# One activation table set for Ln and Exp, a bf16 maximum in the softmax shift, and a new sequence of tasks

## The chip, the cores and the metric

The kernel runs on one core of a Trainium2 chip. The time is that of one execution on the device, in microseconds (us); the profile shows one execution of its own and gives its span, from the first instruction to the last. The engines are PE (matrix products; PEld are its weight loads), DVE (elementwise and reductions), ACT (one function of a table, with scale and bias, per instruction), POOL and SP. SP, POOL and ACT also issue DMAs, each in its own queue. ACT holds one set of function tables at a time; an ACT_TABLE_LOAD instruction changes it, and the program's builder puts one in front of an activation whose function the loaded set lacks.

## The reference

The input x is 2048 rows of 640. Two results are mixed by a gate of each row.

```python
def reference(A_x, A_wqkv, A_wo, ..., B_log_dt, B_Dskip, gate_w):
    # A: attention, 32 heads of 20, each position sees 8 positions at distance 0, 2, ..., 14
    qkv = (x @ wqkv).reshape(B, S, 3, H, Dh)
    logits = einsum("bhsd,bhswd->bhsw", q, kg) * scale
    logits = where(mask, logits, -1e9)
    attn = softmax(logits, axis=-1)
    a = einsum("bhsw,bhswd->bhsd", attn, vg).reshape(B, S, D) @ wo
    # B: a diagonal state space model as a long convolution
    dt = exp(log_dt)[:, None]
    P = exp((dt * A)[:, :, None] * arange(L))       # A complex, 640 x 192
    K = einsum("dn,dnl,dn->dl", Cc, P, dt * Bc).real
    b = irfft(rfft(x padded) * rfft(K padded)) + x * Dskip
    g = sigmoid((x * gate_w).sum(-1))
    return g * a + (1 - g) * b
```

## The kernel before

**Tasks and order.** The work is cut into tasks: 1264 in a plan "main" and 304 in a plan "tail". A task has a name, the engines that can do it, its dependences, and a function that issues its instructions. `ORDER` holds, for each plan, a string of steps from one task's number to the next; a letter after a step (A, D, S, G for ACT, DVE, SP, POOL) chooses the engine where a task may run on two. `Plan.emit` issues the tasks in that sequence, and ties each instruction behind the one before it on its engine. So the string is the program order of every engine and queue, and an engine that waits at a task holds up all that stands behind it. Each task carries a duration for whoever searched the sequence; at run time it has no effect.

**Stages of main.** First (to about 46 us) the parameters. `SSMParams.build` loads C, B, A and log_dt and makes, on [128, 960] tiles, the logarithm of a size and a phase for each of 640 x 192 modes: the products of C and B (`weights`), log and square root by Ln and Exp (`size`, `half`), an arctangent, then a sum (stt_at) and a conversion to integers (fix_t0, L722). Ten results (pieces 0 to 9) are cut to bf16 by tasks mk0 to mk9 and stored to the DRAM tensor Sprm by sp0 to sp9, on SP or POOL. The pieces are tiles pc of a pool of four buffers, taken in turn: the fifth piece made takes the first one's buffer, and so waits until that one's store has landed. When all ten have landed, `KGen.load_L` loads them back as matrices L (queue of SP, the first half also ACT's). In the same stretch SP's queue loads x, wqkv and A; the last two of these loads transpose x (L183) and come, in program order, before any task of SP. PE transposes the other half of x (turn, evicted by tev) and computes q, k and v (late0 to late59, evicted by lev, on ACT or DVE).

Next, the stream (about 46 to 205 us). `KGen.plan` makes K in ten chunks: PE forms angles and exponents (arg, L828), ACT takes the sine (L843) and the exponential (L845), DVE multiplies (pq, L865 and L867), PE sums (kmm, L883). Between them runs attention in eight blocks (`plan_core`): products (prod, L381), logits into PSUM (lg), the maximum over 8 positions (max, L403), its subtraction (neg, L411), the exponential (exp, L415), the sum and division (sum, at), a trip through DRAM to spread the weights (ast, asb on SP), the weighted values (pv, L455), and the output projection (wo, ga). Sine and exponential lie in different table sets, so ACT changes tables between them.

Then K is spread out through DRAM (own, other, then xst and xld on SP and POOL), and the first steps of the Fourier transforms follow: f1 and fk of K, fu of x, each with an eviction of 1024 columns (f1e, fke, fue) from the two PSUM buffers "ar". The tail does the rest of the transforms (fp, sp, products, inv, cp), mixes with the gate and stores.

**The softmax shift.** The logits of a block lie in a PSUM tile lg. DVE takes the maximum mx in f32, and splits -mx into two bf16 tiles, hi (L406) and lo (L407). PE adds both to lg, as two matmuls with the identity (L411). The shift is the same for all 8 positions of a softmax.

Of the kernel before, what the change touches and what calls it, by code (L numbers as in the profile page):

```python
# [11 lines left out]
ALU = mybir.AluOpType  # L12
AX = mybir.AxisListType
F32 = mybir.dt.float32
BF16 = mybir.dt.bfloat16
# [6 lines left out]
D = 640  # L22
# [18 lines left out]
def _attn_consts():  # L41
# [123 lines left out]
class Attn:  # L165
# [86 lines left out]
    def consts(self, cst):  # L252
# [7 lines left out]
        def small():  # L260
            nc.gpsimd.dma_start(self.ind[:], nc.inline_tensor(ind_np, name="c_ind").ap())
            nc.gpsimd.dma_start(self.mask0[:], nc.inline_tensor(mask0_np, name="c_mask0").ap())
# [1171 lines left out]
```

## Time and profile before

| | us |
|---|---|
| three runs | 316.70, 318.62, 317.23 |
| median | 317.23 |
| span of the profiled execution | 315.8 |
| busy PE, DVE, ACT, POOL in it | 288.0, 290.1, 288.5, 55.9 |
| table loads on ACT in it | 18 of 1.283 each |

The profiled execution is not one of the three runs. Its span is 1.4 us below their median; the times of the runs include what lies around the span, and a run differs from the next by up to 1.9 us. Busy means that at least one instruction of the engine was under way; matrix products are pipelined and their ends modelled, so a busy PE isn't PE at its peak. In a timeline row the first two numbers are the start from the span's beginning and the length; a bracket gives the idle time before it and what ended it. SPq and POOLq are the queues in which these engines issue DMAs. In a row of the costliest groups, the numbers behind the bar are busy us, mean ns of one, and idle us before it. In the windows, the columns behind the stretch are its length and the busy us of PE, PEld, DVE, ACT and POOL with the number of instructions, the granted clock of PE, the busy share of the DMA engines and GB/s.

### The profile page before, as it was taken

What the parts mean: (1) busy time and instruction counts of PE and PEld (TensorE: products, weight loads), DVE (VectorE), ACT (ScalarE), POOL (GpSimd) and SP (SyncE); (2) the same over time, 40 slices, a digit from 0 to 9 for tenths busy, and PEclk for the clock granted to TensorE, in tenths of its full rate; (3) what the DMA queues carried; (4) which work ended last, traced back from release to release, by engine and by line L of the source; (5) the groups of instructions that cost most, each with busy time, mean ns of one, the idle gap of its engine ahead of it and who ended that gap; (6) DMA issues with size and microseconds to landing.
All of it is one profiled execution on the core that took longest, in us unless ns stands there. A gap on an engine that the chain in (4) does not pass through costs nothing. (4 is left out here: it accounts for less than half of the span.)

```text
span 315.8 us, 12097 instructions
## 1 busy us (share of the span) xinstructions
PE 288.0 (91%) x5276; PEld 169.2 (54%) x5276; DVE 290.1 (92%) x403; ACT 288.5 (91%) x429; POOL 55.9 (18%) x83
## 2 busy tenths in 40 slices
PE   8899998999999999999998999879989999996840
PEld 3556444445554454546554555446667776656730
DVE  4999999999999999999999999988878799999881
ACT  4999869999999999999999999979987899998890
POOL 8631133200100001111032022040010000000063
PEclk9999999999999999999999999978999999999995
DMA  7995546773412204634698595771192453983066
GB/s 256 366 254 140 153 103 175 167 169 98 91 35 54 69 10 133 130 111 130 187 255 183 110 227 140 139 193 41 66 324 79 153 181 105 196 165 57 4 154 180
DMA packets 47150, 45.67 MB, mean 145 GB/s; under 512 B 27018, under 2 KB 40634, under 8 KB 47098
## 3 DMA queue, kind: packets, MB, share of 16 engines
q1 hardware_dynamic: 40776, 26.68, 33.1%
q0 software_dynamic: 5360, 17.50, 22.1%
q8 instruction: 41, 0.67, 1.0%
q10 hardware_dynamic: 962, 0.73, 0.7%
q14 instruction: 11, 0.09, 0.1%
HBM read 29.57 MB, written 14.01 MB: 138 GB/s over the span
## 5 line engine op out<-in xcount | busy, mean ns | idle before, releaser
L316 PE MATMUL tb<-bufA 128*128 128x512 bf16 x300 | 74.5, 383 | 1.6 <-DMA bufA<-in_A_wqkv_dram 0.8
L843 ACT ACTIVATE big<-ar 128x740 bf16<-128x740 int16 (+1 forms) x72 | 56.9, 858 | 2.4 <-PE ar L828 2.0
L828 PE MATMUL ar<-Rarg,L 64*128 64x212 bf16 (+4 forms) x600 | 48.7, 254 | 4.5 <-ACT big L843 3.0
L845 ACT ACTIVATE big<-ar 128x848 bf16<-128x848 f32 x60 | 50.5, 915 | 0.3 <-PE ar L828 0.2
L455 DVE TENSOR_TENSOR pv<-vc,asb 128x2048 bf16<-128x2048 bf16 x40 | 47.3, 1221 | 1.3 <-DMA asb<-aS 1.3
L316 PEld LDWEIGHTS <-bufA 128*128 128x128 bf16 x300 | 31.7, 120 | 30.0 <-issue 9.1
L828 PEld LDWEIGHTS <-L 64*128 64x128 bf16 x600 | 21.1, 95 | 33.5 <-issue 30.2
L865 DVE TENSOR_TENSOR pt<-big 128x1024 bf16<-128x1024 bf16 x48 | 32.3, 704 | 0.2
L883 PEld LDWEIGHTS <-pt 128*32 128x32 bf16 (+1 forms) x2560 | 23.1, 92 | 11.5 <-issue 8.8
L883 PE MATMUL kps<-qq,pt 128*32 128x21 bf16 (+1 forms) x2560 | 27.8, 175 | 0.8 <-issue 0.8
L486 PE MATMUL tb<-wo_sb,oT 128*128 128x320 bf16 x160 | 27.3, 301 | 0.0
L381 DVE TENSOR_TENSOR prod<-qA,kA 128x2048 bf16<-128x2048 bf16 x20 | 23.6, 1221 | 0.3 <-PE lg L387 0.3
L381 DVE TENSOR_TENSOR prod<-prj 128x2048 bf16<-128x2048 bf16 x20 | 23.8, 1221 | 0.0
L462 PE MATMUL tb<-pv,ind 128*64 128x512 bf16 (+1 forms) x192 | 23.2, 360 | 0.3 <-DVE pv L455 0.3
L513 ACT ACTIVATE sp_k<-fp 128x640 bf16<-128x640 f32 x31 | 22.4, 877 | 0.8 <-PE fp L1096 0.8
L513 ACT ACTIVATE sp_u<-fp 128x640 bf16<-128x640 f32 x29 | 21.6, 894 | 0.2 <-PE fp L1096 0.2
L867 DVE TENSOR_TENSOR qq<-big 128x1344 bf16<-128x1344 bf16 x24 | 21.3, 887 | 0.0
L374 POOL DMA_DIRECT2D vc<-vS x16 | 11.5, 722 | 53.2 <-DVE pv L455 49.0
L1214 POOL DMA_DIRECT2D out_dram<-ot x14 | 7.7, 558 | 69.4 <-ACT tt L1193 68.0
L1096 PEld LDWEIGHTS <-PHI 128*128 128x128 bf16 x160 | 15.5, 97 | 7.8 <-issue 1.3
L486 PEld LDWEIGHTS <-oT 128*128 128x128 bf16 x160 | 13.3, 98 | 8.1 <-issue 3.5
L513 ACT ACTIVATE big<-bp 128x1024 bf16<-128x1024 f32 x14 | 13.9, 1025 | 3.5 <-PE bp L1326 3.3
(177 smaller groups left out, 534.0 us busy)
## 6 DMA issues: line engine op xcount, KB each, us to landing
vc<-vS POOLq DMA_DIRECT2D x16, 327.5 KB, 5.3
gaS<-ga SPq DMA_DIRECT2D x8, 320.0 KB
Usb<-in_A_x_dram POOLq DMA_DIRECT2D x8, 320.0 KB, 4.7
gaF<-gaS SPq DMA_DIRECT2D x8, 320.0 KB
bufA<-in_A_wqkv_dram SPq DMA_DIRECT2D x3, 800.0 KB
L<-Sprm SPq DMA_DIRECT2D x76, 30.0 KB
asb<-aS SPq DMA_DIRECT2D x16, 128.0 KB
psi<-c_psi SPq DMA_DIRECT2D x4, 512.0 KB
```

The lines of the kernel that those rows point to most:

```text
L316: nc.tensor.matmul(ppf, self.wq[:, which, kt, e::5], self.xT[:, c0 // 1024, kt, c0 % 1024:c0 % 1024 + SC], start=(kt == 0), stop=(kt == NK ...
L381: nc.vector.tensor_tensor(b[e][:], q[:, e, o:o + C].unsqueeze(1).to_broadcast([128, W, C]), win(k[:, e, :], o, W, DIL, C), ALU.mult)
L455: nc.vector.tensor_tensor(o, vw, b["asb"][:].unsqueeze(2).to_broadcast(sh), ALU.mult)
L462: nc.tensor.matmul(b["op", e][64 * a:64 * a + 64, 0:n, :], ind[:, 32:96], b["pv", e][:, w, a, 0:n, :], start=(w == 0), stop=(w == 3), skip ...
L486: nc.tensor.matmul(apf[:, :320], b["oT"][:, e, i * 128:(i + 1) * 128], wo_sb[:, e, hf * 320:(hf + 1) * 320], start=(e == 0), stop=(e == 4))
L513: nc.scalar.activation(o, i, ACT.Identity)
L828: nc.tensor.matmul(ar[:, g2, a0:a0 + ncol], L[rows, sb, gv, l0:l0 + 128], R[rows, c0:c0 + ncol], start=True, stop=True, tile_position=(64 ...
L843: nc.scalar.activation(d_[:, :, s0 * QW:s1 * QW], ar[:].bitcast(I16)[:, :, 0:2 * (s1 - s0) * QW:2], ACT.Sin, scale=SCL)
L845: nc.scalar.activation(dst[:, gp::2].rearrange("p g s n -> p g (s n)"), ar[:, :, 0:2 * EW], ACT.Exp)
L865: nc.vector.tensor_tensor(pt[:, :, k, :], gg[:, :, ::-1] if k else gg, e1, ALU.mult)
L867: nc.vector.tensor_tensor(qq[:], trg[:, :, KI:].rearrange("p a (v m) -> p a v m", v=2), exq[:, :, KI:].unsqueeze(2).to_broadcast([128, 32, ...
L883: nc.tensor.matmul(kps[32 * g:32 * g + 32, h, NM * ql:NM * ql + NM], pt[rows, k, v, :], qq[rows, k, v, :], start=(g not in started), stop= ...
```

## The change

Three things are changed.

First, the program loads the set that holds both Ln and Exp before its first activation. The builder keeps a set as long as it serves.

Second, the maximum is written in bf16, and this rounded value is subtracted by one matmul with a negated identity, a constant that is loaded on POOL's queue at the start. A shift that is common to all positions of a softmax cancels, so rounding it does not change the result.

Third, both strings of `ORDER` are new, for the same tasks. The durations that the tasks carry for max and neg are changed with them.

```diff
@@ class Attn: def consts
         self.ident = cst.tile([128, 128], BF16, name="ident")
+        self.minus = cst.tile([128, 128], BF16, name="minus")
...
             nc.gpsimd.dma_start(self.mask0[:], nc.inline_tensor(mask0_np, name="c_mask0").ap())
+            nc.gpsimd.dma_start(self.minus[:], nc.inline_tensor((-ident_np.astype(np.float32)).astype(NPBF), name="c_minus").ap())
@@ class Attn: def plan_core
-                mx = wk.tile([128, 64], F32, name="mx", bufs=1)
-                nc.vector.tensor_reduce(mx[:], lg[:].rearrange("p w t -> p t w"), AX.X, ALU.max)
-                b["hi"] = wk.tile([128, 64], BF16, name="hi", bufs=1)
-                b["lo"] = wk.tile([128, 64], BF16, name="lo", bufs=1)
-                nc.vector.tensor_scalar(b["hi"][:], mx[:], -1.0, None, ALU.mult)
-                nc.vector.scalar_tensor_tensor(b["lo"][:], mx[:], -1.0, b["hi"][:], ALU.mult, ALU.subtract)
+                b["mx"] = wk.tile([128, 64], BF16, name="mx", bufs=1)
+                nc.vector.tensor_reduce(b["mx"][:], lg[:].rearrange("p w t -> p t w"), AX.X, ALU.max)
...
-                for k in ("hi", "lo"):
-                    nc.tensor.matmul(b["lg"][:], ident[:], b[k][:].unsqueeze(1).to_broadcast([128, W, 64]), start=False, stop=(k == "lo"), skip_group_check=True)
+                nc.tensor.matmul(b["lg"][:], self.minus[:], b["mx"][:].unsqueeze(1).to_broadcast([128, W, 64]), start=False, stop=True, skip_group_check=True)
...
-            mx = pl.add(f"max{sc}", "D", 1.09, top, deps=[l])
-            ng = pl.add(f"neg{sc}", "P", 0.435, lower, deps=[mx], eq=1024)
+            mx = pl.add(f"max{sc}", "D", 0.65 if sc else 0.9, top, deps=[l])
+            ng = pl.add(f"neg{sc}", "P", 0.216, lower, deps=[mx], eq=512)
@@ class SSMParams: def build
         lnd = pin.tile([128, 5], F32, name="lnd")
+        nc.scalar.preload_act_table_set("natural_log_exp_and_others")
         nc.scalar.activation(dtb[:], ldt[:], ACT.Exp)
```

The strings are long and can't be read as they stand. Decoded with the tasks' numbers, the sequence of the parameter stage is, on ACT and DVE from the start to the first sine (act00000), and on SP and POOL for the first tasks:

```
ACT before: lnd tev2 tev0 tev1 act_ax act_xa lev0 act_xl lev1 tev3 lev3 lev2 act_xl(Ln) act_ay(Exp) tev5 lev10 lev7
            act_t0(Ln) act_t1(Exp) lev12 act_at(Arctan) lin_t1 lev6 mk1 lev20 mk0 lev30 lev18 mk6 lev11 mk7 kh1 lev19
            lev16 gexp lev25 L0A gtwice exp0 wsin act00000
ACT after:  lnd act_xl tev2 tev0 tev1 act_xa act_ax lev0 act_xl(Ln) act_ay(Exp) lev3 tev3 lev2 mk3 lev5 tev4 lev4
            act_t0(Ln) act_t1(Exp) lev14 tev5 lev12 mk2 act_at(Arctan) lev9 lev6 mk1 lev15 mk0 lev20 lev7 mk7 kh1 mk6
            gexp lev11 lev18 lev30 L0A lev19 lev25 gtwice exp0 act00000
DVE before: wr t0 t1 wi wi wr by_tau near_x1 tau fix_s1 mk2 xl mk3 tev4 lev5 kh0 lev4 by_xa ay stt_xl lev13 lev15 mk4
            lev8 mk8 lev14 t1 lev9 mk5 mk9 stt_t1 stt_at stt_at fix_t0 prod00 ... prod04 gsig max0
DVE after:  wr t0 wr wi t1 wi by_tau xl near_x1 lev1 tau fix_s1 ay stt_xl mk8 mk9 lev10 by_xa mk4 t1 lev8 lev13 mk5
            lin_t1 stt_t1 stt_at stt_at fix_t0 kh0 prod00 prod01 prod02 gsig prod03 prod04 lev16 max0
SP before:  sp4 sp5 sp0 sp6 sp7 L0S L1 ast0 asb0 ast1 L2
SP after:   sp3 sp8 sp7 sp6 L0S L1 ast0 asb0 L2 ast1 asb1
POOL before: sp2 sp3 dskip sp8 sp9 sp1 gst consts
POOL after:  consts sp9 sp4 sp2 sp5 dskip sp1 sp0 wo
```

In the whole of main, ACT has 317 tasks after and 312 before, DVE 259 and 264; 25 tasks go from DVE to ACT and 20 from ACT to DVE (nine evictions lev and four fue each way; beside them mk2, mk3, tev4, four ga, two fin, oT14, fke0 and fke1h0 to ACT, and lin_t1, two ga, oT24, oT62, fke2 and fke7h0 to DVE). wsin, a sine of one column that brought in the sine's tables, moves behind the last sine. Of the ten f1 tasks seven now stand behind the last sine and three in chunk 9; before, three stood behind it, three in chunk 9 and four in chunks 7 and 8. On SP, xld0 follows xst0 at once; before, ast5 stood between them. In the tail six evictions go each way (sp and cp tasks), and the order within its stages is new.

88 rows, old and new, of the table ORDER are left out of this document.

## The prediction, made before the changed kernel ran

> **What bounds the kernel now.** I read the page's busy line first, then the windows by stage, then the costliest groups for what the diff touches, and last the timelines of ACT, DVE and SP up to the first sine.
>
> ```profile
> span 315.8 us, 12097 instructions
> PE 288.0 (91%) x5276; PEld 169.2 (54%) x5276; DVE 290.1 (92%) x403; ACT 288.5 (91%) x429; POOL 55.9 (18%) x83
> ...
> 0.00:16.00 16.00, 13.21 (x71) 6.61 (x72) 11.71 (x18) 10.63 (x17) 12.44 (x18) 1.00 0.94 311
> 16.00:30.00 14.00, 14.00 (x78) 7.75 (x75) 13.61 (x19) 13.45 (x16) 3.51 (x5) 1.00 0.92 205
> 30.00:50.00 20.00, 19.14 (x196) 9.84 (x194) 19.10 (x26) 16.27 (x25) 4.71 (x7) 1.00 0.54 146
> 50.00:100.00 50.00, 49.22 (x1143) 25.75 (x1139) 48.39 (x65) 49.71 (x71) 6.23 (x9) 1.00 0.50 110
> 100.00:150.00 50.00, 49.76 (x1174) 25.61 (x1163) 49.23 (x76) 49.78 (x74) 4.63 (x6) 1.00 0.36 92
> 150.00:200.00 50.00, 48.14 (x1014) 26.63 (x1012) 49.04 (x59) 49.47 (x80) 10.25 (x14) 1.00 0.77 183
> 200.00:245.00 45.00, 40.15 (x787) 26.68 (x787) 38.89 (x56) 39.39 (x53) 6.40 (x11) 0.92 0.45 138
> ```
>
> No engine stands out by its share (all three at 91 to 92%). The windows (columns: stretch, length, then busy PE, PEld, DVE, ACT, POOL, clock, DMA share, GB/s) are more use. From 50 to 200 ACT is full, 148.96 of 150 us, and DVE nearly, 146.66. Before 50 and after 200 both have holes: from 30 to 50 ACT works 16.27 of 20, from 200 to 245 DVE and ACT lack 6.1 and 5.6 us. So work taken off DVE or ACT counts only if the holes do not grow, and in the stream it is ACT that must lose work. The span is 1.4 us below the median of 317.23; I make the sum as a difference and add it to that median.
>
> **The change part by part: what goes.**
>
> ```profile
> L406 DVE TENSOR_SCALAR hi<-mx 128x64 bf16<-128x64 f32 x8 | 1.6, 195 | 0.3
> L407 DVE SCALAR_TENSOR_TENSOR lo<-mx,hi 128x64 bf16<-128x64 f32 x8 | 1.8, 225 | 0.3
> L411 PE MATMUL lg<-lo,ident 128*128 128x512 bf16 x8 | 3.0, 379 | 0.0
> ```
>
> Maximum: the two DVE steps go, 8 x (0.195 + 0.225) = 3.36 us. The reduction stays and writes bf16 instead of f32, 64 elements a row; costed at nothing. One of two matmuls goes: 8 x 0.38 = 3.0 us of PE at most.
>
> ```profile
> 6.29 1.28 ACT L705 ACT_TABLE_LOAD   x1
> ...
> 17.89 1.28 ACT L708 ACT_TABLE_LOAD   x1
> 19.19 1.01 ACT L708 ACTIVATE ay<-xl 128x960 f32<-128x960 f32 x1
> ...
> 21.89 1.28 ACT L710 ACT_TABLE_LOAD   x1
> 23.19 1.10 ACT L710 ACTIVATE t<-ay,bc 128x960 f32<-128x960 f32 x1
> 24.30 1.28 ACT L711 ACT_TABLE_LOAD   x1
> 25.60 1.01 ACT L711 ACTIVATE t<-t 128x960 f32<-128x960 f32 x1
> ...
> 27.50 1.28 ACT L653 ACT_TABLE_LOAD   x1
> 28.79 1.00 ACT L653 ACTIVATE at<-t 128x960 f32<-128x960 f32 x1
> 29.83 1.09 ACT L660 ACTIVATE t<-at,bc 128x960 f32<-128x960 f32 x1
> ```
>
> Tables: with one set for Ln and Exp the loads at L705, L708, L710 and L711 go; the first (at L608) becomes the preload, the one for Arctan stays. Decoding the order string shows five exp-to-sin and sin-to-exp pairs later, as before. So 18 loads become 14: 4 x 1.28 = 5.13 us of ACT, three of them on the serial path from L704 to the arctangent.
>
> The Trainium skill ("ScalarE: Activation LUTs", section "What ACT_TABLE_LOAD costs") puts a switch at about 2.66 us with a drain. By that figure four would be 10.6 us. The rows disagree: L711's load starts at 24.30 and its ACTIVATE at 25.60, 1.30 in all; I keep 1.28.
>
> **What moves between DVE and ACT.** In the main plan 25 tasks go from DVE to ACT and 20 back. Most pair off by kind. Net on ACT: mk2 and mk3 (pieces of the phase), tev4 (a 128x1024 eviction) and three small evictions, less lin_t1.
>
> ```profile
> L729 DVE TENSOR_SCALAR pc<-s 128x960 bf16<-128x960 uint8 x2 | 1.3, 657 | 0.0
> L731 ACT ACTIVATE pc<-s 128x960 bf16<-128x960 uint8 x1 | 1.0, 991 | 0.0
> L513 ACT ACTIVATE bufA<-ar 128x1024 bf16<-128x1024 f32 x3 | 3.0, 1028 | 0.0
> L515 DVE CAST bufA<-ar 128x1024 bf16<-128x1024 f32 x1 | 1.2, 1219 | 0.0
> L495 ACT ACTIVATE ga<-tb,g_sb 128x320 bf16<-128x320 f32 x24 | 12.9, 568 | 0.1
> ...
> 34.54 0.66 DVE L722 TENSOR_SCALAR t<-at 128x960 int32<-128x960 f32 x1
> ```
>
> ACT gains 2 x 0.99 + 1.03 + 3 x 0.57 - 1.09 = 3.6 us. DVE loses 2 x 0.66 + 1.22 + 3 x 0.55 - 0.66 = 3.5 us (0.66 for lin_t1 from the like-sized L722). Altogether ACT is 5.13 - 3.6 = 1.5 us lighter, DVE 3.36 + 3.5 = 6.9 us. Nearly all of the moved work lies before the first sine; behind it ACT has about 0.7 us more than before and DVE 3.4 us less. An even use of this would give (1.5 + 6.9)/2 = 4.2 us.
>
> **The front: a wait in place of the loads.** The saved loads shorten the path only if ACT can run on. In the new sequence ACT does ... Ln, Exp, evictions, mk3, ..., Ln, Exp, lev14, tev5, lev12, **mk2**, Arctan. The pieces rotate through four buffers (tile pc), and the new order of pieces is mk3, mk8, mk9, mk4, mk2: mk2 needs mk3's buffer, free once the store sp3 has landed. And sp3 moves from POOL's queue to SP's, behind the two transposing loads.
>
> ```profile
> 4.47 1.16 DVE L635 TENSOR_TENSOR wr<-cre,bre 128x960 f32<-128x960 bf16 x1 [3.25 <-DMA bre<-in_B_B_re_dram]
> ...
> 10.00 1.15 DVE L635 TENSOR_TENSOR wr<-wr,t 128x960 f32<-128x960 f32 x1
> ...
> 9.92 13.85 SPq L183 DMA_TRANSPOSE bufA<-in_A_x_dram  x2
> 24.86 13.39 SPq L674 DMA_DIRECT2D Sprm<-pc  x5
> ...
> DMA to landing us min/median/max: 2.9/3.8/6.2
> ```
>
> SP is held by the transposes until 9.92 + 13.85 = 23.77, whatever is ready earlier. The landing (tile pc, the stores from POOL; SP's own aren't shown) takes 2.9 to 6.2, median 3.8. So mk2 starts at 23.8 + 3.8 = 27.6, from 26.7 to 30.0. ACT would reach it sooner: in the new order DVE has eight 128x960 operations before Ln can start; now the sixth of them starts at 10.00, a pitch of (10.00 - 4.47)/5 = 1.1, so they end at 4.5 + 8 x 1.1 = 13.3; Ln and Exp then end at 15.6; seven evictions and mk3 take it to about 20.3, the second pair to 22.4, three evictions to 24.0. The wait is 3.6 us and eats most of the 3.85 us won on the path.
>
> Then: mk2 27.6 to 28.6, the load to 29.9, Arctan to 30.9, against 29.79 now: 1.1 later. lin_t1 on DVE (0.66 for 1.09) gives 0.4 back. mk5 on DVE waits for sp8 in the same way, but what stands behind it on DVE needs the arctangent anyhow.
>
> ```profile
> 36.62 1.08 ACT L731 ACTIVATE pc<-t,bc 128x960 bf16<-128x960 uint16 x1
> ...
> 40.57 5.21 SPq L793 DMA_DIRECT2D L<-Sprm  x12
> ...
> 43.91 0.60 ACT L415 ACTIVATE at<-lg 128x512 bf16<-128x512 f32 x1 [0.27 <-PE lg L411]
> 44.53 1.28 ACT L750 ACT_TABLE_LOAD   x1
> 46.50 6.59 ACT L843 ACTIVATE big<-ar 128x888 bf16<-128x888 int16 x9 [0.48 <-PE ar L828]
> ```
>
> From there the path is as now: the last conversion L722 (ends 35.2, new 35.8), the last two pieces (now until 37.7, new 38.2 with the halo copy between them), their stores, the load of L from 40.57, the first sine at 46.50. Front: **+0.5 us**. Bounds: with no wait, mk2 at 24.0, 3.6 earlier than that, **-3.1**; with the landing at 6.2, mk2 at 30.0, 2.4 later, **+2.9**.
>
> **The rest.** Behind the first sine ACT is full and has no less to do, DVE 3.4 us less. Bounds: +0.7 (ACT alone sets the pace) and -3.4 (DVE alone). ACT's row is nearer to full, so I take a quarter: **-0.8**.
>
> ```profile
> L1033 POOL DMA_DIRECT2D F1c<-c_f x1 | 0.6, 582 | 0.0
> ...
> 210.00:215.00 5.00, 4.49 (x88) 2.41 (x88) 5.00 (x6) 3.42 (x5) 0.00 (x0) 0.50 0.67 183
> ```
>
> From 200 on, the sequence is new as well: seven of the ten f1 evictions (1 us each) stand behind the last sine, where three stood, so the K part ends sooner with more left to cover its store and reload. Against that, these evictions share two PSUM buffers with the twenty of fu. In the window's row the clock is at half and ACT idles 1.58 us; a new sequence may or may not have it. Bounds -1.6 and +1.5; half of the idle taken: **-0.8**. The Trainium skill ("TensorE: Matmul & The Clock Gate", section "What's actually happening") says that low activity of TensorE halves its clock; the row shows such a stretch, and no run here shows what sets it off.
>
> The tail's twelve swaps are six each way: 0, bounds +-1. Hidden: the load of the negated identity (one POOL issue ahead of the buffer memsets) and the three consts issues moved to the front, since POOL is busy only 3.51 of 14 us from 16 to 30; without that cover, 4 x 0.58 = 2.3 us on POOL's stores. On SP, xld0 now follows xst0 at once and waits for its landing with L8 and ast5 behind; L8 is wanted a K chunk later.
>
> Sum: +0.5 - 0.8 - 0.8 = -1.1; 317.2 - 1.1 = **316.1 us**.
>
> **The rivals.** *The front's gain survives.* If mk2 does not wait (sp3 lands sooner than SP's row lets me believe, or ACT comes to it late), the front is -3.1 and the time 317.2 - 3.1 - 1.6 = **312.5**. For it: 8.4 us of ACT and DVE work really goes. Against it: the row 9.92 + 13.85.
>
> *The store comes later still (slower).* If sp3's completion queues behind the transposes' data, mk2 starts at 30.0 or later; ACT, full from the first sine on, can't win it back: 317.2 + 2.9 + 0.7 = **320.8**. It decides from a landing of about 6 us on (slower by over 1% begins at 320.4). The Trainium skill ("DMA: Bandwidth & Descriptors", section "Queues, rings and completion order") says that a completion is signalled only after every earlier write of the same DMA engine, which speaks for this case; no row of before shows when an SP store lands. Against it: the landing's median, 3.8.
>
> *The table part does nothing.* If the combined set did not serve both functions, all 18 loads would stay and ACT would reach mk2 at 24.0 + 3 x 1.28 = 27.8 instead of waiting until 27.6: **316.3**.
>
> **How the numbers follow.** The wait at mk2 with 316.1 I give 0.60, the loads staying 0.03: both within 1% (314.1 to 320.4, about what a measurement of this kernel can tell from no change). The surviving gain 0.28: faster by over 1%. The late store 0.09, slower. Range: 312.3 to 319.3, from just under the surviving gain (312.5) to the forecast with the late landing of 2.4 more and 0.8 of the late part lost.
>
> **What would show it.** Right: an ACT pause before L731 (mk2) that ends near 27.6, SP's first store at 23.8, Arctan near 29.9, the first sine near 47, 14 loads, no lo tile, ACT still the fullest from 50 to 200. Wrong: Arctan before 28, the first sine before 45, or a stretch from 200 to the tail that is shorter by more than 2 us. A half clock in another place would shift the sum by 1 to 2 us either way.

## The result, and the profile after

The changed kernel takes 337.23 us (median of 4 runs, 335.87 to 339.4) against 317.77 us of the kernel before on the same chip: a ratio of 1.0596, 95% interval 1.0548 to 1.0644. The prediction was 316.1 us, with a range from 312.3 to 319.3 and a chance of 0.09 for slower. It was wrong by 21 us and in its sign. The profiled execution spans 334.1 us, 18.3 more than before. The ratios leave out executions more than 1.5% above the fastest of the same kernel (the medians keep them), and the trace of the run called "wo later" below is of such an execution, so that its marks are rough.

Busy line and windows of the changed kernel, read as those before (stretch, length, busy PE, PEld, DVE, ACT, POOL, clock, DMA share, GB/s):

```profile
span 334.1 us, 12064 instructions
PE 287.6 (86%) x5242; PEld 169.3 (51%) x5268; DVE 285.2 (85%) x382; ACT 286.2 (86%) x430; POOL 57.8 (17%) x85
...
0.00:16.00 16.00, 13.39 (x67) 6.49 (x69) 11.49 (x17) 9.73 (x16) 14.70 (x21) 1.00 0.94 311
16.00:30.00 14.00, 11.49 (x60) 6.28 (x60) 10.71 (x13) 8.73 (x14) 1.80 (x3) 1.00 1.19 222
30.00:50.00 20.00, 16.06 (x148) 8.15 (x149) 15.33 (x20) 13.44 (x21) 7.13 (x10) 0.83 0.63 159
50.00:100.00 50.00, 45.49 (x855) 21.64 (x862) 42.11 (x54) 45.85 (x63) 5.04 (x8) 0.97 0.42 92
100.00:150.00 50.00, 46.79 (x1126) 25.56 (x1139) 47.39 (x65) 48.05 (x71) 2.31 (x3) 1.00 0.21 52
150.00:200.00 50.00, 45.76 (x1144) 25.22 (x1148) 46.84 (x61) 48.44 (x76) 8.92 (x12) 1.00 0.73 182
200.00:245.00 45.00, 36.99 (x814) 23.04 (x811) 35.14 (x51) 37.34 (x57) 9.46 (x15) 0.93 0.55 141
```

The work did go: DVE is busy 4.9 us less and ACT 2.3 us less than before, and there are 14 table loads. What grew is idle time, on all three engines and in every stretch from 16 on. From 50 to 200 ACT now works 45.85 + 48.05 + 48.44 = 142.3 of 150 us (148.96 before) and DVE 136.3 (146.66 before). That ACT is full in this stretch, from which the prediction took its bounds there, no longer holds.

The rows of ACT and DVE, taken in order, are the tasks of the sequence. Three marks show where the time came from: the start of the first sine, the start of the last eviction that DVE makes in the main plan (called the end of main below), and the end of the span.

| | before | after | more |
|---|---|---|---|
| first sine starts | 46.50 | 52.53 | 6.0 |
| from there to the last eviction of main | 200.9 | 212.5 | 11.6 |
| from there to the end of the span | 68.4 | 69.1 | 0.7 |

So a third is lost in the front, nearly all the rest between the first sine and the end of main. Each mark is of one execution: in four traces with the changed kernel's front the first sine starts between 52.53 and 53.96. (In the expectations below, act00000 is the row 0.8 us behind the first sine: 47.3 before, 53.3 after.)

Timelines of ACT and of SP's queue in the front of the changed kernel, two lines of its waits (who waited for whom: total, times, longest), ACT's part of the load of L and the first sine, its windows from 24 to 36, and the same two windows of the kernel before:

```profile
23.59 0.60 ACT L512 ACTIVATE pv<-tb 128x512 bf16<-128x512 f32 x1
29.43 1.00 ACT L731 ACTIVATE pc<-s 128x960 bf16<-128x960 uint8 x1 [5.23 <-DMA Sprm<-pc]
30.45 1.28 ACT L653 ACT_TABLE_LOAD   x1
31.74 1.00 ACT L653 ACTIVATE at<-t 128x960 f32<-128x960 f32 x1
...
9.85 15.40 SPq L185 DMA_TRANSPOSE bufA<-in_A_x_dram  x2
25.37 16.35 SPq L674 DMA_DIRECT2D Sprm<-pc  x4
...
PE tb L320 <- ACT kA L512: 5.5, 1, 5.5
ACT pc L731 <- DMA Sprm<-pc: 5.2, 1, 5.2
...
47.44 1.51 ACTq L793 DMA_DIRECT2D L<-Sprm  x4
52.53 1.59 ACT L843 ACTIVATE big<-ar 128x888 bf16<-128x888 int16 x2 [0.54 <-PE ar L828]
...
24.00:30.00 6.00, 3.75 (x18) 1.91 (x17) 2.85 (x4) 0.77 (x2) 0.37 (x1) 1.00 0.97 252
30.00:36.00 6.00, 2.72 (x7) 1.00 (x7) 3.12 (x4) 4.97 (x7) 3.72 (x5) 0.52 0.31 82
...
24.00:30.00 6.00, 6.00 (x33) 3.22 (x30) 5.79 (x9) 5.63 (x7) 0.89 (x1) 1.00 0.56 140
30.00:36.00 6.00, 6.00 (x100) 4.11 (x99) 5.73 (x6) 5.53 (x8) 1.69 (x2) 1.00 0.63 166
```

The wait at mk2 is there as predicted: ACT arrives at 24.2 (predicted 24.0), SP is held until 25.25 (23.8), the first store is issued at 25.37 and has landed when mk2 starts at 29.43 (27.6). What the prediction did not follow comes next. Behind the waiting ACT stand the evictions that free PSUM for the projection, so PE waits 5.5 us for ACT. In 24 to 36 PE works 3.75 + 2.72 us, at 0.52 of its clock in the second half; before it worked 12.00 of these 12 us at full clock. And the pieces come late as well: Arctan 2.95 us later than before, SP's last store 3.5 us (41.20 for 37.73), ACT's part of the load of L, which waits for all ten stores, 6.8 us (47.44 for 40.63), the first sine 6.0.

### The profile page after: what moved, and what is told of

Same layout as the page of the kernel before. It is cut to its first block, busy times and chain, and to the rows that moved or that the text cites. A ratio compares the mean times of both kernels' runs of the same rounds, so it can differ in the third digit from the quotient of the medians.

```text
span 334.1 us, 12064 instructions
## 1 busy us (share of the span) xinstructions
PE 287.6 (86%) x5242; PEld 169.3 (51%) x5268; DVE 285.2 (85%) x382; ACT 286.2 (86%) x430; POOL 57.8 (17%) x85
## 5 line engine op out<-in xcount | busy, mean ns | idle before, releaser
L843 ACT ACTIVATE big<-ar 128x740 bf16<-128x740 int16 (+1 forms) x72 | 55.8, 848 | 0.9 <-PE ar L828 0.8
L883 PE MATMUL kps<-qq,pt 128*32 128x21 bf16 (+1 forms) x2560 | 28.5, 174 | 4.9 <-issue 4.9
L461 PE MATMUL tb<-pv,ind 128*64 128x512 bf16 (+1 forms) x192 | 24.7, 367 | 4.1 <-DVE pv L454 3.2
L378 POOL DMA_DIRECT2D vc<-vS x16 | 11.6, 741 | 46.6 <-DVE pv L454 38.6
L485 PEld LDWEIGHTS <-oT 128*128 128x128 bf16 x160 | 13.7, 98 | 7.7 <-issue 2.9
L843 ACT ACTIVATE bufA<-ar 128x740 bf16<-128x740 int16 (+1 forms) x18 | 14.5, 847 | 1.7 <-PE ar L828 1.4
```

What stands on the lines that cost most here:

```text
L461: nc.tensor.matmul(b["op", e][64 * a:64 * a + 64, 0:n, :], ind[:, 32:96], b["pv", e][:, w, a, 0:n, :], start=(w == 0), stop=(w == 3), skip ...
L485: nc.tensor.matmul(apf[:, :320], b["oT"][:, e, i * 128:(i + 1) * 128], wo_sb[:, e, hf * 320:(hf + 1) * 320], start=(e == 0), stop=(e == 4))
L843: nc.scalar.activation(d_[:, :, s0 * QW:s1 * QW], ar[:].bitcast(I16)[:, :, 0:2 * (s1 - s0) * QW:2], ACT.Sin, scale=SCL)
L883: nc.tensor.matmul(kps[32 * g:32 * g + 32, h, NM * ql:NM * ql + NM], pt[rows, k, v, :], qq[rows, k, v, :], start=(g not in started), stop= ...
```

## The experiments

Ratios are to the kernel before in the same batch of runs, with 95% intervals. "Old" and "new" sequence are those before and after the change.

### The edits apart from the sequences

```diff
 e2: code of after
-ORDER = new main, new tail
+ORDER = old main, old tail
 e8: before, with only
+nc.scalar.preload_act_table_set("natural_log_exp_and_others")
 e14: before, with only
+nc.vector.tensor_reduce(b["mx"][:] (BF16), ...)
+nc.tensor.matmul(b["lg"][:], self.minus[:], b["mx"]..., start=False, stop=True, ...)
```

> The changed kernel's code (one table set, maximum in bf16, one lowering matmul) with both sequences of the kernel before. Theory Q (all of the loss is the sequences', and the edits themselves gain): the loads at L705, L708, L710, L711 are gone, Arctan comes up to 3.85 us earlier than 28.8, and the time is 312.5 to 316.5 us against 317.8. Rival E (the edits themselves cost, for instance by the pace at which the old sequence then meets its stores): 318 or more. If the edits are hidden: 317 to 318.

> The kernel before with the preload of the common table set alone; maximum and sequences as before. The loads at L705, L708, L710 and L711 go (4 x 1.28 us of ACT). If DVE's order sets the front (theory D: in the run with the old sequences ACT idled 2.99 us before the eviction ahead of Arctan and Arctan came at 28.95), Arctan stays within 0.3 us of 28.8, the first sine within 0.7 us of 46.5, and the time is 316.5 to 318, the rest of that run's gain (2.2 us in the medians) being the maximum's on DVE. If the tables are the gain: 315 to 316.5.

> The kernel before with the change of the maximum alone (reduction to bf16, no remainder, one lowering matmul with the negated identity); tables and sequences as before. The tables alone measured 1.0054 of the kernel before, both edits together 0.9932. Theory M (the gain is the maximum's: DVE loses 3.36 us in the full stretch): 314.5 to 316.5, ratio 0.990 to 0.995. Rival: the two only gain together, or what differs is where the pauses and half-clock stretches of PE fall: 317 to 319, ratio 0.998 to 1.004.

| | ratio | first sine | end of main |
|---|---|---|---|
| before | 1 | 46.50 | 247.38 |
| both edits, old sequences | 0.9932 [0.9896, 0.9968] | 45.90 | 245.54 |
| tables alone | 1.0054 [1.0011, 1.0098] | 46.62 | 250.46 |
| maximum alone | 0.9926 [0.9881, 0.9971] | 46.15 | 246.07 |

Theory Q holds: with the old sequences the edits gain 0.7% (316.14 us, expected 312.5 to 316.5), so the sequences hold the whole loss. The gain is the maximum's (315.97 us alone, expected 314.5 to 316.5). The tables gain nothing although 18 loads become 14: 319.94 us, expected 316.5 to 318. That they cost half a per cent by themselves is at the edge of the interval, and the cause was not followed. Why the front gains nothing shows in the run with both edits: ACT around the arctangent, then a window.

```profile
23.05 1.00 ACT L709 ACTIVATE t<-t 128x960 f32<-128x960 f32 x1
27.05 0.60 ACT L510 ACTIVATE pv<-tb 128x512 bf16<-128x512 f32 x1 [2.99 <-PE tb L318]
27.66 1.28 ACT L651 ACT_TABLE_LOAD   x1
28.95 1.01 ACT L651 ACTIVATE at<-t 128x960 f32<-128x960 f32 x1
...
24.00:30.00 6.00, 6.00 (x29) 3.26 (x28) 5.66 (x9) 2.95 (x5) 0.89 (x1) 1.00 0.52 129
```

Exp is done 2.55 us sooner than before (25.60 then), and the arctangent is not: ACT stands 2.99 us at an eviction, for a matmul. From 24 to 30 PE works 6.00 of 6.00 us and ACT 2.95. With the tables alone it is the same: 2.99 us at this eviction, Arctan at 28.91.

### The front

```diff
 e3:  +old main up to the first sine, then the tasks left in the new order
 e1:  -sp3, sp8 on SP           +sp3, sp8 on POOL, same places
 e6:  ACT: -mk2 act_at lev9 lev6     +act_at lev9 lev6 mk2
      DVE: -mk5 ... fix_t0           +... fix_t0 mk5
 e11: POOL: -wo lst02 vc0 lst12      +lst02 vc0 lst12 wo
 e13: -tc.tile_pool(name="sp_pc", bufs=4, side="right")
      +tc.tile_pool(name="sp_pc", bufs=7, side="right")
```

> The changed kernel's code; the sequence is that of the kernel before up to and including the first sine (act00000), the tasks left follow in the new order, the tail is the new one. Theory F: first sine at 43 to 46 instead of 52.5, and the time falls by at least those 6 to 9 us, to 328 to 331; what is left of the loss (10 us or more against 317.8) is the new stream and late part. Rival S: above 335. If the front is at the root of all of it: below 322.

> The changed kernel (337.2 us) with one thing undone: the stores sp3 and sp8 are issued by POOL again, at the same places of the sequence, instead of by SP behind its two transposing loads. Theory F (the front's wait at mk2 is a cause of its own): mk3 ends at 18.8, its store lands some 4 us later, so mk2 follows the evictions before it at about 24.2 without a pause, Arctan starts near 26.5 instead of 31.7, the first sine near 46.5 or before instead of 52.5, and the time falls by 6 us or more, to 331 or less; if the half clock from 30 to 50 and the idle time of the stream hang on it too, to about 326. Rival S (the delay is taken up later, by idle time that the new sequence has in any case): the pause at mk2 goes, but the time stays above 335.

> The changed kernel with two pieces of the phase moved, stores left on SP: mk2 goes on ACT from before the arctangent to behind it and two evictions, mk5 on DVE from before the first product with the arctangent to behind the last conversion. So neither Arctan nor the conversions wait for a store that lands late. Theory F (the front's 5.5 us are the waits of these two pieces, and carry through to the end): Arctan near 25.5, conversion near 32, first sine at 47 to 49 instead of 52.5, and the time falls by 4 to 6 us, to 331 to 333. Rival S (the projection's matmuls on PE, or the load of L behind wo's, set the first sine anyway): first sine after 51, time 335.5 or more.

> The changed kernel with one task moved on POOL's queue: wo, the load of the output weights (800 KB in two issues), from ahead of the load of L to behind lst12, where the kernel before has it. In the runs with wo at 36.6 to 39.2, SP's load of L waits 4.6 to 4.9 us for the last piece's store, against 1.5 in the kernel before, whatever was done about the pieces. Theory O (wo's transfer holds up the last stores): that wait falls to about 1.5 to 2.5, the first sine comes 2 to 3 us sooner (49.5 to 50.5 by the trace's 52.5 to 54) and the time falls by 2 to 3 us, to 334 to 335. Rival: the wait is the stores' own number in flight, and the first sine stays behind 52.

> The changed kernel, order untouched, with seven buffers instead of four for the pieces of the phase (tile pc). Then mk2, mk5, mk1 and mk0 wait for no store or for one that left long before. Theory F2 (the front is lost by waits of ACT and DVE for piece buffers: behind ACT's wait stand the evictions that free PSUM for the projection, PE stops and goes to half clock, and the projection is late): ACT reaches mk2 at about 24.2 without a pause, Arctan starts near 26.5, PE keeps full clock from 30 to 50, the first sine comes at 46 to 48.5 instead of 53.3, and the time falls by 5 to 7 us, to 330 to 332. Rival G (PE's order of the projection in the new sequence sets the first sine whatever the pieces do): first sine after 51.5, time 335 or more.

| | ratio | first sine | end of main |
|---|---|---|---|
| after | 1.0596 [1.0548, 1.0644] | 52.53 | 264.99 |
| old front, new rest | 1.0401 [1.0332, 1.0470] | 46.06 | 259.54 |
| sp3, sp8 on POOL | 1.0625 [1.0547, 1.0704] | 52.95 | 265.60 |
| two pieces later | 1.0621 [1.0554, 1.0688] | 52.71 | 266.84 |
| wo later | 1.0607 [1.0498, 1.0716] | 54.84 | 270.50 |
| seven buffers | 1.0345 [1.0270, 1.0421] | 47.77 | 261.92 |

The old front brings 5.5 us at the end of main: the front's delay is carried through almost whole (332.59 us, expected 328 to 331). But three of four attempts at its cause left the time where it was or above (339.04, 337.15 and 340.32 us; expected: 331 or less, 331 to 333 and 334 to 335), each in a telling way. Of the stores on POOL: median landing by the DMA view of the stores issued from 19 to 30 us and from 27 to 45 us, then rows of ACT and DVE.

```profile
Sprm<-pc POOLq DMA_DIRECT2D x5, 240.0 KB, 10.2
...
Sprm<-pc POOLq DMA_DIRECT2D x4, 240.0 KB, 3.2
...
26.38 1.00 ACT L731 ACTIVATE pc<-s 128x960 bf16<-128x960 uint8 x1 [2.12 <-DMA Sprm<-pc]
31.87 1.16 DVE L677 TENSOR_TENSOR pc<-xa,pc 128x960 bf16<-128x960 f32 x1 [5.48 <-DMA Sprm<-pc]
```

Issued earlier, the stores do not land in time: five of them, issued while the transposing loads ran or just after, take 10.2 us (median), four later ones 3.2. The transposing loads alone are not the reason: in the changed kernel a store that POOL issued beside them at 23.54 had landed after 5.0 us, with fewer stores under way. ACT's wait shrinks from 5.23 to 2.12, DVE's at the next piece (mk5) grows from 1.53 to 5.48, and the conversions come no sooner. The rule of the Trainium skill ("DMA: Bandwidth & Descriptors", section "Queues, rings and completion order"), that a completion is signalled only after every earlier write of the same DMA engine, agrees with this; that the engines were simply shared fits as well, and no run here parts the two.

With mk2 and mk5 behind the arctangent, Arctan starts at 25.56, and the waits move on: waits of that run.

```profile
ACT pc L731 <- DMA Sprm<-pc: 5.9, 2, 4.0
...
DVE pc L677 <- DMA Sprm<-pc: 3.0, 1, 3.0
```

Ten pieces go through four buffers; putting one later only makes another one wait. The last conversion ends at 31.53 (37.73 in the changed kernel), but the load of L goes out no sooner (ACT's part at 47.62), and rival S had the first sine right.

Of the run with wo later, theory O was right about its wait (SP's load of L waited 1.2 us for the last store instead of 4.6) and wrong about the time. In the changed kernel the first sine does stand behind L: it starts 5.09 us after ACT issues its part, and 5.09 to 5.10 us in the runs with two pieces later and with seven buffers too. With the last store landing sooner, ACT comes to that part later than SP does (48.20 for 45.95), behind an eviction that waits for PE, and the first sine starts 6.64 us after it; so it is with the stores on POOL (46.31, 6.64). Two holds lie close together here, the last store and the projection's evictions, and shortening one leaves the other. Seven buffers, with the order untouched, relieve both. ACT of that run, then its windows:

```profile
24.34 1.01 ACT L731 ACTIVATE pc<-s 128x960 bf16<-128x960 uint8 x1
25.38 1.28 ACT L653 ACT_TABLE_LOAD   x1
26.67 1.01 ACT L653 ACTIVATE at<-t 128x960 f32<-128x960 f32 x1
...
16.00:30.00 14.00, 13.62 (x72) 7.41 (x70) 13.12 (x16) 13.94 (x20) 4.54 (x7) 1.00 1.23 206
30.00:50.00 20.00, 19.00 (x187) 9.63 (x185) 16.21 (x24) 12.40 (x20) 5.08 (x7) 0.91 0.87 211
```

No pause at mk2, Arctan at 26.67 (expected 26.5), PE busy 13.62 and 19.00 us instead of 11.49 and 16.06, the first sine 4.8 us sooner, the median at 331.3 (expected 330 to 332). Theory F2 stands: the front is lost by waiting for piece buffers. How much of it goes by way of PE and how much by way of the pieces themselves these runs don't part: with seven buffers ACT's part of L also goes out 4.8 us sooner (42.67). What is left, 1.3 us at the first sine against the kernel before, holds a wait of SP for the last store again (its last store goes out at 35.70, L at 42.70); seven buffers with wo later were not tried.

### The stream

```diff
 e7:  PE: -kmm102 kmm103 kmm110 kmm111 kmm112 kmm113 arg2101
      PE: +kmm102 arg2101 kmm103 late38 kmm110 ...   (every row of kmm from act10000 on)
 e15: e2 with its kmm spread in the same way
 e9, e10: as e3, but the old sequence up to act30000, up to act60000
```

> The changed kernel with the same tasks on the same engines; only the short matmuls into kps (L883) are spread: where several tasks of them stand in a row on PE, the later ones are put one by one behind the next other matmuls. In the traces so far PE pauses (put down to issue) at the same instruction counts in all runs of this sequence, always at a multiple of 256 instructions (matmuls and weight loads, less a constant 74 to 89), where the 256 before it ran in 1.2 to 3.1 us: 2.09 us at 89.98, 1.45 at 153.97, 1.39 at 229.22, with the clock at half for some 4 us behind the first. Theory B (PE's instructions come in blocks of 256 and a block takes over 3 us to come; bunched short matmuls run it dry): with no 256 in less than 3.2 us the pauses at 90 and 154 are gone, ACT and DVE wait 3 to 6 us less between 50 and 200, and the time falls by 3 to 7 us, to 330 to 334. Rival N (the pauses are no cause; the stream waits because of where the sine arguments stand between the projection's matmuls): 335.5 or more.

> The changed kernel's code with both sequences of the kernel before and the short matmuls into kps spread among the others. With the old sequences PE made one pause at such a block of 256 instructions in the main plan (1.14 us at 162.0). Theory B: that pause goes, 0.5 to 1.5 us of the end with it: 314.5 to 316, ratio 0.988 to 0.993, the fastest of all. Rival: the spread matmuls delay what waits for kps, or a block falls elsewhere: 316 to 318.

> The changed kernel's code with the sequence of the kernel before up to act30000 (98.9 us into the run with the old sequences), the rest in the new order, new tail. With the cut at the first sine the main plan ended 14.0 us later than with the old sequences all through (259.5 against 245.5). Theory P (the new order loses in the first half of the stream, where it still has the projection's matmuls between the sine arguments on PE, and the rest only carries it on): the end falls to 248 to 252, the span to 316 to 320. Rival U (the loss accrues evenly, some 5 us in each third): 254 to 256. Rival Z (it is the second half): 257 to 260.

> As the run before, with the cut at act60000 (138.9 us into the run with the old sequences). Theory P: no further gain, the main plan ends at 246 to 250. Rival U: 250 to 252. Rival Z: 254 or later, so that the last part alone holds more than 8 of the 14 us.

PE of the changed kernel, and the windows around:

```profile
86.61 1.27 PE L883 MATMUL kps<-qq,pt 128*32 128x21 bf16 x135
89.98 0.33 PE L883 MATMUL kps<-qq,pt 64*32 64x21 bf16 x25 [2.09 <-issue]
...
88.00:90.00 2.00, 0.02 (x4) 0.02 (x6) 2.00 (x3) 0.96 (x1) 0.00 (x0) 1.00 0.00 0
90.00:92.00 2.00, 1.82 (x38) 1.13 (x39) 1.56 (x2) 1.36 (x2) 0.14 (x1) 0.91 0.03 8
92.00:94.00 2.00, 2.00 (x9) 0.57 (x8) 0.00 (x0) 1.25 (x3) 1.80 (x3) 0.50 0.32 57
94.00:96.00 2.00, 2.00 (x15) 0.52 (x13) 1.03 (x2) 1.13 (x2) 0.00 (x0) 0.74 1.08 245
96.00:98.00 2.00, 2.00 (x39) 0.91 (x35) 1.41 (x2) 1.89 (x4) 0.00 (x0) 1.00 0.43 74
```

After 135 short matmuls in 1.27 us PE stands still for 2.09 us though the profile shows nothing that it waits for, and then runs at half clock; DVE does nothing from 92 to 94. With the matmuls spread the pauses at 90 and 154 are gone, and 50 to 100 reads:

```profile
50.00:100.00 50.00, 45.91 (x863) 22.46 (x875) 43.87 (x57) 47.70 (x65) 5.63 (x8) 1.00 0.43 96
```

The clock stays at 1.00, ACT works 1.85 us more in this window, DVE 1.76. From 50 to 200 ACT idles 2.4 us less and DVE 1.5 (expected 3 to 6). Yet the median is 336.77 us, ratio 1.0600 [1.0563, 1.0637]: not told apart from the change, as rival N had it. This run's first sine came 1.4 us later (its store landed later; the same code gave mk2 between 29.4 and 30.5 in the runs that share this front), and from the first sine to the end of main it is 1.6 us shorter. Theory B is right that these two pauses go with the rows, and was too high about their worth. In the old sequence the same spreading costs: 323.83 us, 1.0181 [1.0132, 1.0231], main's end 7.6 us later than without it, where both theories had 318 or less; and PE still pauses once for 1.14 us, now at 176 instead of 162. So a row of short matmuls is not bad in itself. That spreading delays what waits for kps is likely but was not followed.

The cuts did not find one place. With the old sequence up to act30000 main ended at 261.84 (332.11 us, one run), later than with the cut at the first sine (259.54); up to act60000 at 254.11 (324.67 us, one run), still 8.6 us behind the old sequence all through, as rival Z had it. Theory P falls. But the first of these keeps more of the old sequence than the cut at the first sine and ends later, and ACT idles 5.6 us from 100 to 150 behind its seam; if a seam has a price of its own, such cuts are poor evidence for any of the three.

### The late part

```diff
 e4: DVE: -shift1 own1 other1 pv62 pv62b pv64    +pv62 pv62b shift1 own1 other1 pv64
 e5: new main up to act90210, then the 191 tasks left as in the old order
```

> The changed kernel with two tasks moved on DVE alone: pv62 and pv62b, the products of values and probabilities for the attention of chunk 6, go ahead of shift1 and own1, the copies into X that wait for all ten f1 matmuls. Theory L (own1's wait for the f1 matmuls, 5.7 us of DVE, delays the attention behind it, and that sets the end of the late part): DVE works 2.3 us of those 5.7, PE's wait of 2.7 and ACT's of 4.8 us shrink by as much, and the time falls by 2 to 4 us, to 333 to 335. Rival K (the end of the late part is set by X's store and reload for the K part): no change, 336.5 to 338. The front is untouched, so more than 5 us less would speak against both.

> The changed kernel with its new sequence up to the last sine (act90210); the 191 tasks of the main plan that are left then follow in the order, and on the engines, of the kernel before; the tail is the new one. Theory L (the late part's new order loses by itself, above all where own1 stands on DVE ahead of the products of chunks 6 and 7): the 34.4 us from fin9 to the last eviction of the main plan shrink to about 28, and the time falls by 5 to 7 us, to 330 to 332. Rival W (the late part is longer only because the stream leaves more work to it): no more than 2 us, 335 or more.

The kernel before, DVE at own1 (L930); then the changed kernel, DVE, PE and ACT around it:

```profile
224.68 1.68 DVE L930 COPY X<-E 128x640 bf16<-128x640 bf16 x8
...
236.53 1.67 DVE L930 COPY X<-E 128x640 bf16<-128x640 bf16 x8 [5.69 <-PE bp L1330]
...
240.03 0.59 PE L461 MATMUL tb<-pv,ind 128*64 128x512 bf16 x1 [2.69 <-DVE pv L454]
...
243.92 0.38 ACT L512 ACTIVATE oT<-tb 128x256 bf16<-128x256 f32 x1 [4.84 <-PE tb L461]
```

own1 writes X over the buffer that the ten f1 matmuls read, so it waits for all ten; the products for the attention stand behind it on DVE, PE waits for them, ACT for PE. In the kernel before own1 did not wait. With two products ahead of own1 the ratio is 1.0515 [1.0459, 1.0570], 335.81 us (expected 333 to 335), its interval just overlapping that of the change, and from the first sine to the end of main it is 2.4 us less; own1 itself still waits 5.37 us. Theory L has the direction and part of the size. The old order for the whole late part does not help: 339.91 us, 1.0704 [1.0657, 1.0752], expected 330 to 332. Rival W, that the new stream leaves more work to the late part, fits this; why it is slower than the change was not followed.

### Together, and a better version

> The changed kernel's code and new order with three repairs at once: the old order up to the first sine, the short matmuls into kps spread, and the products of chunk 6 (pv62, pv62b) ahead of own1. Single prices by the idle time of ACT from the first sine to the end of the main plan: spreading 2.5 us, products 2.9 us; the old front 6 us. Theory A (they add): the main plan ends near 259.5 - 2.5 - 3 = 254, the time is 322 to 325 and some 8 us of the stream's loss stay without a name. Rival M (the waits mask each other, so the repairs together give more than their sum): 319 or less. Rival: spreading is worth nothing again, 327 or more.

> The changed kernel with its new order and three repairs that leave that order's front in place: seven piece buffers, the short matmuls into kps spread, the products of chunk 6 ahead of own1. With the old front in place of the buffers the same measured 325.4 us (main plan's end 253.5). Theory F2: 324 to 327. If the buffers do not repair the front (rival G): 330 or more.

Old front, spreading and products together: 1.0245 [1.0175, 1.0316], 325.44 us (expected 322 to 325), main's end at 253.47, 6.07 us sooner than with the old front alone (expected 5.5). Seven buffers in place of the old front: 1.0224 [1.0165, 1.0284], 326.1 us (expected 324 to 327). At main's end the repairs add, or a little more: spreading and products gave 1.6 and 2.4 us there by themselves, counted from the first sine.

```diff
 e17: e2, and in the front  DVE: -lev8 mk8 lev14 t1   +t1 mk8
                            ACT: -act_t1 lev12 act_at +act_t1 lev8 lev14 lev12 act_at
 e18: e17 with bufs=7 for sp_pc
```

> The changed kernel's code with the sequences of the kernel before, and in its front two evictions (lev8, lev14) on ACT instead of DVE and the product for Arctan (t1) ahead of them and of mk8 on DVE. Theory D (DVE's order kept the saved table loads from counting): Arctan at 26.5 to 27.3 instead of 28.95, the conversion 1.6 to 2.4 us sooner, the first sine 1 to 2 us sooner (45 to 45.7 by act00000's 46.7 now) and the time 314 to 315.5, ratio 0.985 to 0.991. Rival P2 (PE, which is full from 24 to 42, sets the first sine): Arctan sooner, first sine within 0.5 us of 46.7, time 315.5 to 317.

> As the run before, with seven buffers for the pieces of the phase. Theory D: the same as that run within 0.5 us, as the old order waits for no piece buffer. If the pieces had become the next hold: first sine 0.5 to 1.5 us sooner than in that run and the time as much less. Rival P2: first sine within 0.5 us of 46.7 again.

Neither is faster than the run that they start from: 0.9977 [0.9942, 1.0013] and 0.9966 [0.9928, 1.0003]. ACT of the first:

```profile
26.30 0.60 ACT L510 ACTIVATE kA<-tb 128x512 bf16<-128x512 f32 x1 [0.83 <-PE tb L318]
27.38 0.60 ACT L510 ACTIVATE pv<-tb 128x512 bf16<-128x512 f32 x1 [0.48 <-PE tb L318]
28.46 0.60 ACT L510 ACTIVATE pv<-tb 128x512 bf16<-128x512 f32 x1 [0.48 <-PE tb L318]
...
30.37 1.00 ACT L651 ACTIVATE at<-t 128x960 f32<-128x960 f32 x1
```

Three evictions, one every 1.08 us, each waiting for PE. Arctan starts 4.90 us after Exp has ended, as in the run that it starts from (24.05 and 28.95) and with seven buffers (24.11 and 29.01). That the rows above lie 1.4 us later is no effect of the edit: this trace is as much behind at the first Exp, ahead of the edited places (19.49 for 18.07), and with seven buffers the first sine starts at 46.07. So the product is not what Arctan stands behind; PE, busy 6.00 of 6.00 us from 24 to 30 with seven buffers, sets its pace (rival P2, which had expected Arctan sooner; it came no sooner). This fits the table part's gaining nothing in this front. The versions that beat both kernels are the maximum alone (315.97 us) and both edits with the old sequences (316.14 us).

## Why the prediction was wrong, point by point

In main's end, before to after, the 17.6 us come apart as: edits with the old sequences -1.8; new order from the first sine on +14.0 (old front run against old sequences), of which spreading the short matmuls and moving the products ahead of own1 give back 6.1; new front +5.5. Each figure is the difference of two traces.

- **The table loads, -5.13 us of ACT.** The loads went, 18 to 14, as counted. The step that failed is that three of them shorten the path: in the old front they became waiting for PE (2.99 us), which the prediction's own window had at 14.00 of 14 us from 16 to 30. The prediction read the holes of ACT and DVE in these windows, and not that PE has none.
- **The maximum, -3.36 us of DVE.** Right. The reduction takes 686 ns with a bf16 result and took 688 with f32, and alone the change takes the time to 0.9926.
- **The front, +0.5 us.** The mechanism was right up to Arctan (mk2 behind sp3 behind the transposes), every time of it within 2 us: 24.2 for 24.0, 25.37 for 23.8, 29.43 for 27.6, 31.74 for 29.9. One size was off: the transposes held SP 15.40 us and not 13.85, why was not followed. The step that failed is the next one, "from there the path is as now". It left out the evictions queued on ACT behind mk2 and PE behind these, and it left out that the load of wo now runs ahead of the last stores: Arctan came 2.95 us later than before, the load of L 6.8, the first sine 6.0. "Late store" had the right sign and place; its 320.8 lacked the same step.
- **The stream, -0.8, bounds +0.7 and -3.4.** This failed altogether. The bounds took the old sequence's fullness for a property of the work. ACT was full because in that sequence its operands were nearly always ready (1.0 us idle in 50 to 200); the new one leaves ACT 7.7 us and DVE 13.7 us idle there. From the first sine to the end of main it takes 11.6 us more, for -0.8 here and -0.8 in the late stage. No row of before could bound that, and a range that held such an outcome would have been the honest one.
- **The late stage, -0.8.** Failed at "the K part ends sooner with more left to cover its store and reload": the deferred f1 evictions were counted as cover, and the decoded order had own1, which depends on all ten f1, ahead of the products. The dependence was in the code, and the prediction did not hold the new place of own1 against it: DVE waited 5.69 us there, ACT behind it 4.84.
- **The tail, 0 within 1.** Right: 0.7.
- **The table rival.** Decided: 14 loads, the common set serves both functions.

Open: 7.9 us of the new order (main's end of the three repairs, 253.47, against 245.54). ACT is idle there 11.7 us from the first sine on against 6.2, most of the difference from 50 to 150, and busy 2.4 us longer. No wait of ACT there is above 1.6 us; DVE still waits 4.2 us at own1, which no run took away. No run settles it.

## What to carry to other kernels

A wait on one engine is priced by what is queued behind it, and then by who waits for that: here taking away a wait of 5.2 us on ACT, behind which stood PSUM evictions and the rest of the pieces, gave back 4.8 us at the first sine. A new order of everything is not the sum of its edits: keep the order fixed, measure the edits, and change the order by itself. Where a buffer rotation waits, more buffers test the cause at once, while moving single users only moves the wait.

## What the runs showed of the hardware

- PE pauses at fixed counts. In all eight traces that keep the new order's rows of short matmuls PE paused at the same two places, after 1974 to 1985 and 4778 to 4801 recorded instructions (matmuls, weight loads and a few semaphore instructions; pauses of 1.45 to 2.48 us); the changed kernel also after 6823 and 8103 (0.89 and 1.39 us). From the first on the distances are 2804, 2045 and 1280, close to 11, 8 and 5 times 256 (a few records are missing in a trace). In the five traces with the most records (the kernel before, the maximum alone, seven buffers, the old order spread, the repaired new order) the eight pauses from 50 to 245 us that are above 0.4 us and put down to issue all come after a multiple of 256 plus 193. The 256 records before each of the changed kernel's four took 1.2 to 3.1 us, but before some others 4.2 to 8.2 us, so that a short block alone does not make the pause. The Trainium skill ("Runtime: NRT & Kernel Launch", section "Instruction fetch mechanics") says that code is fetched in blocks of 256 instructions and that this is hidden by the issue rate. The block agrees with the counts; that the fetch is what PE waits for is not shown, but if it is, it is not hidden behind 135 matmuls in 1.27 us.
- A pause of PE of 2.09 us was followed by some 4 us at a lower clock (0.50 from 92 to 94, 0.74 from 94 to 96). The prediction had said that no run shows what sets this off; here it comes behind a pause, and goes when the pause goes. It does not always come: of the 16 pauses at the two places in those eight traces 14 were followed within 8 us by a stretch at 0.50, and two were not (1.45 us in the changed kernel at 154, 1.75 us with the stores on POOL at 90).
- Five stores of 240 KB issued by POOL between 19 and 30 us, most of them beside two transposing loads, took 10.2 us to land (median); four issued between 27 and 45 us took 3.2.
